# Row block 4 of a Gram matrix on column tiles, behind the K stage; z on four tiles of its own

## The chip, the cores and the metric

One core of a Trainium2 chip. The metric is the device time of one execution in microseconds (us). The profile shows one execution, by its span (about 1.7 us shorter than the time measured for the same execution).

## The reference, cut to what matters

`x` is 2048 x 576; its layer norm `xn` feeds an attention block without softmax and a gated feed-forward block, and both results are added to `x`:

```python
q, k, v = ...(xn @ wqkv)                         # 32 heads of 18
pq, pk = phi(q), phi(k)                          # phi(t) = (t + 1 if t > 0 else exp(t)) + 1e-6
kv = jnp.einsum("bhsd,bhse->bhde", pk, v)
z = jnp.einsum("bhsd->bhd", pk)                  # sums of pk over the sequence
num = jnp.einsum("bhqd,bhde->bhqe", pq, kv)
den = jnp.einsum("bhqd,bhd->bhq", pq, z)[..., None] + 1e-6
o = num / den                                    # then @ wo
return x + attention(xn) + (gelu(xn @ w_gate) * (xn @ w_up)) @ w_down
```

The kernel never forms `v`. It accumulates the Gram product `G = xn^T pk` (576 x 576) over the 16 sequence tiles and multiplies it by the v weights once, in the "kv stage". `z` is the column sum of `pk`.

## The kernel before

576 is 4.5 times 128, so G has four row blocks of 128 rows and a fifth, number 4, of 64. A column of ones appended to `xn` adds a 65th row to block 4, and that row is z. Blocks 0, 1 and 4 accumulate inside the K loop, block 2 behind it, and block 3 after q unit 12 (a q unit is five matmuls of 512 columns that make a piece of q, with the ScalarE and VectorE steps that follow):

```python
G_A = {
    0: [(0, 0, 0, 288), (1, 0, 288, 289)],          # (bank, first column in bank, first column of pk, width)
    1: [(2, 0, 0, 288), (3, 0, 288, 289)],
    4: [(0, 288, 0, 224), (1, 289, 224, 223), (2, 288, 447, 130)],
}
G_B = {2: [(5, 0, 0, 288), (6, 0, 288, 289)], 3: [(0, 0, 0, 288), (1, 0, 288, 289)]}

def g_accumulate(n, pieces):
    for kt, ps_ in pieces.items():
        j0, m = (kt * P, P) if kt < 4 else (D, HP + 1)
        for b, col, d0, w in ps_:
            nc.tensor.matmul(ps_all[:m, b, col:col + w], lhsT=xn[:, n, j0:j0 + m], rhs=pk[:, n, d0:d0 + w], ...)
# ... the K loop, which runs g_accumulate(n, G_A), cut ...
for n in range(NS):
    g_accumulate(n, {2: G_B[2]})
# ... copies of blocks 4, 0 and 1 out of PSUM, the remaining q steps, cut ...
q_unit(12)
# ...
for n in range(NS):
    g_accumulate(n, {3: G_B[3]})
g_copy(2, G_B, (nc.scalar, nc.vector))
g_copy(3, G_B, (nc.scalar, nc.vector))
q_unit(13)
z_stage(2, 3)      # 5 matmuls that spread z over the rows of zrep
kv_stage(6, 5)     # 25 matmuls: v weights times G
```

All products live in one tensor, `ps_all`, of 8 banks in PSUM, the memory that the matmuls write and the copies read. The layer that places the semaphores makes two engines that use the same bank take turns, whatever part of the bank each of them uses; the waits in the built programs show it.

Of the kernel before, what the change touches and what calls it, by code (L numbers as in the profile page):

```python
# [8 lines left out]
ACT = mybir.ActivationFunctionType  # L9
ALU = mybir.AluOpType  # L10
BF16 = mybir.dt.bfloat16
F32 = mybir.dt.float32
# [3 lines left out]
P = 128  # L16
HP = 64
S = 2048
D = 576
# [3 lines left out]
NS = S // P  # L23
# [4 lines left out]
HALF = D // 2  # L28
KT = 5
# [3 lines left out]
CR = 7 * DH  # L33
EPS_LN = 1e-5
EPS_ATT = 1e-6
# [2 lines left out]
WDS = 3  # L38
NWARM = 38
TD = 4  # L40
XW = 642
PKW = 578


class _Ring:
# [11 lines left out]
def kernel(  # L57
# [11 lines left out]
    nc = tc.nc  # L69
# [8 lines left out]
    const = ctx.enter_context(tc.tile_pool(name="const", bufs=1))  # L78
# [6 lines left out]
    ps_all = psum.tile([P, 8, 512], F32, name="ps_all")  # L85
# [10 lines left out]
    apool = attn_cm.__enter__()  # L96
# [5 lines left out]
    wqkv_sb = apool.tile([P, KT, 3 * D], BF16, name="wqkv_sb")  # L102
# [4 lines left out]
    def load_w(which, on=nc.sync):  # L107
        c = slice(which * D, (which + 1) * D)
        on.dma_start(wqkv_sb[:, 0:4, c], A_wqkv[0:512, c].rearrange("(kt p) c -> p kt c", p=P))
        on.dma_start(wqkv_sb[0:HP, 4, c], A_wqkv[512:576, c])  # L110
        if which == 0:
            on.dma_start(wq_lo[HP:P, :], A_wqkv[512:576, c])

    nc.scalar.preload_act_table_set("natural_log_exp_and_others")  # L114
    load_x(0, 1)
# [3 lines left out]
    nc.vector.memset(wqkv_sb[HP:P, 4, :], 0.0)  # L119
    nc.vector.memset(wqkv_sb[0:1, 0, D:D + 2], 0.0)  # L120
    load_w(1, nc.scalar)

    ident = const.tile([P, P], BF16, name="ident")
# [29 lines left out]

    pk = h_store[:, 0:NS * PKW].rearrange("p (n d) -> p n d", n=NS)
    wg_bufs = _Ring([fpool.tile([P, 4, GUB * P], BF16, name=f"wg{i}") for i in range(NWBUF)])
# [5 lines left out]
    def load_gu(i, part):  # L161
# [15 lines left out]


    xn = apool.tile([P, NS, XW], BF16, name="xn")
    nc.gpsimd.memset(xn[:, :, 640:641], 1.0)  # L180
    nc.gpsimd.memset(pk[:, :, D:D + 1], 1.0)

    bmask = const.tile([P, CR], F32, name="bmask")
    bm3 = bmask[:].rearrange("p (h e) -> p h e", e=DH)
# [2 lines left out]
        out=bm3, in_=bm3, compare_op=ALU.is_ge, fill=0.0,  # L187
# [3 lines left out]
        out=bm3, in_=bm3, compare_op=ALU.is_ge, fill=0.0,  # L191
        base=DH - 1, pattern=[[DH, 7], [0, DH]], channel_multiplier=-1,
    )
    g_sb = apool.tile([P, KT, D], BF16, name="g_sb")
    nc.gpsimd.memset(g_sb[HP:P, 4, :], 0.0)

    zsel = const.tile([P, CR], BF16, name="zsel")
    nc.gpsimd.memset(zsel[:], 0.0)
    nc.gpsimd.memset(zsel[HP:HP + 1, :], 1.0)

    mv = persist.tile([P, NS, nc.vector.BN_AGGR_DIM], F32, name="mv")
    rstd = persist.tile([P, NS], F32, name="rstd")
# [36 lines left out]
    def k_bank(n, hf):  # L239

        return hf if n == 1 else 5 + hf
# [9 lines left out]
    def phi_tile():  # L251
        return awork.tile([P, D], F32, name="phi_e", tag="phi_e", bufs=6)


    k_e = {}

    def k_part(n, hf):
        if n not in k_e:
            k_e[n] = phi_tile()
        hs = slice(hf * HALF, (hf + 1) * HALF)  # L260
        return ps_all[:, k_bank(n, hf), :HALF], k_e[n][:, hs], pk[:, n, hs]

    def k_relu(n, hf):
        ps, e, _ = k_part(n, hf)
        nc.scalar.activation(out=e, in_=ps, func=ACT.Relu, scale=-1.0)  # L265

    def k_exp(n, hf):
        _, e, _ = k_part(n, hf)
        nc.scalar.activation(out=e, in_=e, func=ACT.Exp, scale=-1.0)  # L269

    def k_sum(n, hf):
        ps, e, out_ = k_part(n, hf)
        nc.vector.scalar_tensor_tensor(out=out_, in0=ps, scalar=0.0, in1=e, op0=ALU.max, op1=ALU.add)  # L273
# [1 line left out]


    G_A = {
        0: [(0, 0, 0, 288), (1, 0, 288, 289)],
        1: [(2, 0, 0, 288), (3, 0, 288, 289)],
        4: [(0, 288, 0, 224), (1, 289, 224, 223), (2, 288, 447, 130)],  # L280
    }
    G_B = {2: [(5, 0, 0, 288), (6, 0, 288, 289)], 3: [(0, 0, 0, 288), (1, 0, 288, 289)]}
    eps_sum = const.tile([P, KT], F32, name="eps_sum")

    def g_accumulate(n, pieces):
        for kt, ps_ in pieces.items():
            j0, m = (kt * P, P) if kt < 4 else (D, HP + 1)
            for b, col, d0, w in ps_:
                nc.tensor.matmul(  # L289
                    ps_all[:m, b, col:col + w], lhsT=xn[:, n, j0:j0 + m], rhs=pk[:, n, d0:d0 + w],  # L290
                    start=(n == 0 and col == 0), stop=(n == NS - 1), skip_group_check=True,
                )



# [2 lines left out]
    LO, HI = slice(0, HP), slice(HP, P)  # L298
# [37 lines left out]
    def q_unit(i):  # L336
        sc, c = divmod(i, NCH)
        rows = DH * HCH[c]
        q0 = DH * HOFF[c]
        ps = ps_all[:rows, q_banks.next(), :]  # L340
        for kt in range(KT):
            nc.tensor.matmul(  # L342
                ps, lhsT=wqkv_sb[:, kt, q0:q0 + rows], rhs=xnT[:, kt, sc * SC:(sc + 1) * SC],
                start=(kt == 0), stop=(kt == KT - 1),
            )
        q_out[i] = ps
# [57 lines left out]
    def mask_pair(dst, b4, b1):  # L404

        nc.vector.tensor_tensor(
            out=dst[:CR, 0:4, :], in0=ps_all[:CR, b4, 0:4 * CR].rearrange("p (c d) -> p c d", c=4),
            in1=bmask[:CR, :].unsqueeze(1).to_broadcast([CR, 4, CR]), op=ALU.mult,
        )
        r4 = DH * HCH[4]  # L410
        nc.vector.tensor_tensor(
            out=dst[:r4, 4, :r4], in0=ps_all[:r4, b1, 0:r4], in1=bmask[:r4, :r4], op=ALU.mult,
        )

    def chunk_out(c, b4, b1):
        rows = DH * HCH[c]
        return ps_all[:rows, b4, c * CR:c * CR + rows] if c < 4 else ps_all[:rows, b1, 0:rows]

    def z_stage(b4, b1):
        for c in range(NCH):  # L420
            rows = DH * HCH[c]
            nc.tensor.matmul(
                chunk_out(c, b4, b1), lhsT=g_sb[:, 4, c * CR:c * CR + rows], rhs=zsel[:, :rows],
                start=(c in (0, 4)), stop=True, skip_group_check=True,
            )
        mask_pair(zrep, b4, b1)

    def kv_stage(b4, b1):

        for kt in (0, 1, 4, 2, 3):  # L430
            for c in range(NCH):
                rows = DH * HCH[c]
                nc.tensor.matmul(  # L433
                    chunk_out(c, b4, b1), lhsT=wqkv_sb[:, kt, 2 * D + c * CR:2 * D + c * CR + rows],
                    rhs=g_sb[:, kt, c * CR:c * CR + rows],
                    start=(kt == 0 and c in (0, 4)), stop=(kt == 3), skip_group_check=True,
                )
        mask_pair(kvT, b4, b1)

# [29 lines left out]
    def den_norm(sc, c, q, pieces):  # L469
# [30 lines left out]
        (lambda n: k_sum(n, 0), [9.00, 16.55, 13.07, 15.61, 18.43, 21.08, 23.93, 26.99, 30.05]),  # L500
        (lambda n: k_sum(n, 1), [10.83, 11.19, 13.68, 16.19, 18.79, 21.44, 24.29, 27.35, 30.41]),
        (lambda n: g_accumulate(n, G_A), [11.96, 17.36, 18.24, 20.21, 21.09, 23.07, 26.12, 29.18, 32.24]),
    ]

# [27 lines left out]
    todo += [(4.0, lambda n: nc.vector.memset(x_sb[0:1, n, 0:2], 0.0), 4)]  # L532
    todo += [(4.01, lambda n: load_x(n, 4), n) for n in (4,)]
    todo += [(4.02, lambda n: load_w(0), 0)] + [(4.03, lambda n: load_x(n, 4), n) for n in (8, 12)]
    todo.sort(key=lambda x: x[0])

# [2 lines left out]
        step(n)  # L539


    def g_copy(kt, pieces, on):

        m = P if kt < 4 else HP + 1
        eps = eps_sum[:m, kt:kt + 1]
        b, col, _, w = pieces[kt][-1]
        nc.vector.tensor_scalar_mul(out=eps, in0=ps_all[:m, b, col + w - 1:col + w], scalar1=EPS_ATT)
        for (b, col, d0, w), eng in zip(pieces[kt][::-1], on):
            w = min(w, D - d0)
            out_, in_ = g_sb[:m, kt, d0:d0 + w], ps_all[:m, b, col:col + w]  # L550
            if eng is nc.scalar:
                nc.scalar.activation(out=out_, in_=in_, func=ACT.Identity, bias=eps, scale=1.0)
            else:
                nc.vector.tensor_scalar_add(out=out_, in0=in_, scalar1=eps)


    load_w(2)
    for i in range(NWBUF):
        load_gu(i, 0)
        load_gu(i, 1)  # L560
    for n in range(NS):
        g_accumulate(n, {2: G_B[2]})
    g_copy(4, G_A, (nc.vector, nc.scalar, nc.vector))
    g_copy(0, G_A, (nc.scalar, nc.vector))
    g_copy(1, G_A, (nc.scalar, nc.vector))
    for _, step, n in todo[tail:]:
        step(n)
    q_unit(12)
    for step in (q_exp1, q_min, q_max):
        step(12)  # L570
    for n in range(NS):
        g_accumulate(n, {3: G_B[3]})
    g_copy(2, G_B, (nc.scalar, nc.vector))
    g_copy(3, G_B, (nc.scalar, nc.vector))
    q_unit(13)
    z_stage(2, 3)
    kv_stage(6, 5)
    for step in (q_exp1, q_min, q_max):
        step(13)
# [161 lines left out]
```

## Time and profile before

| what | before |
|---|---|
| time, first series | 523.57 us (523.47 to 523.83, 3 runs) |
| TensorE busy | 99% of the span |
| stage: end of q unit 11 to end of the kv stage | 53.20 to 65.78, 12.58 us |
| of it, 32 Gram matmuls behind the K loop, and 32 more behind q unit 12 | 4.00 us each |
| TensorE idle in the stage | none |

The stage is read from the chain of waits: the pieces of the chain in order of time, with start, length, engine, tile and line.

### The profile page before, as it was taken

What the parts mean: (1) busy time and instruction counts of PE and PEld (TensorE: products, weight loads), DVE (VectorE), ACT (ScalarE), POOL (GpSimd) and SP (SyncE); (2) the same over time, 40 slices, a digit from 0 to 9 for tenths busy, and PEclk for the clock granted to TensorE, in tenths of its full rate; (3) what the DMA queues carried; (4) which work ended last, traced back from release to release, by engine and by line L of the source; (5) the groups of instructions that cost most, each with busy time, mean ns of one, the idle gap of its engine ahead of it and who ended that gap; (6) DMA issues with size and microseconds to landing.
All of it is one profiled execution on the core that took longest, in us unless ns stands there. A gap on an engine that the chain in (4) does not pass through costs nothing.

```text
span 521.7 us, 10641 instructions
## 1 busy us (share of the span) xinstructions
PE 516.1 (99%) x4498; PEld 313.5 (60%) x4498; DVE 250.9 (48%) x436; ACT 143.1 (27%) x293; POOL 35.2 (7%) x55
## 2 busy tenths in 40 slices
PE   7999999999999999999999999999999999999997
PEld 6777755555587754444577744444777544445775
DVE  7996565876358323433388133333584233433101
ACT  6898442332320013323200032232000123322000
POOL 2021000211001100000012000000011000000000
PEclk9999999999999999999999999999999999999999
DMA  8334609899500045555300155555100355440000
GB/s 279 62 64 118 154 25 264 254 269 266 157 12 13 13 124 155 144 156 160 93 13 13 41 166 145 155 156 155 29 23 13 103 161 158 140 134 2 13 11 24
DMA packets 106282, 57.89 MB, mean 111 GB/s; under 512 B 13370, under 2 KB 105722, under 8 KB 106234
## 3 DMA queue, kind: packets, MB, share of 16 engines
q1 hardware_dynamic: 105626, 56.55, 38.8%
q8 instruction: 35, 0.57, 0.5%
q10 hardware_dynamic: 608, 0.66, 0.4%
q14 instruction: 13, 0.11, 0.1%
HBM read 52.86 MB, written 2.36 MB: 106 GB/s over the span
## 4 chain that ended last, share of the span: by engine, by line
PE 97%; DMA 1%; ACT 1%; DVE 0%; issue 0%
PE ps_all L313 55%; PE ps_all L677 27%; PE ps_all L289 4%; PE ps_all L682 4%; PE ps_all L245 3%; PE ps_all L342 3%; DMA wqkv_sb<-in_A_wqkv_dram 1%; PE ps_all L451 1%; PE ps_all L433 0%; PE ps_all L659 0%; ACT xnT L234 0%; ACT L114 0%; ACT phi_e L265 0%; ACT phi_e L269 0%; DVE hT L273 0%; DVE res L685 0%
## 5 line engine op out<-in xcount | busy, mean ns | idle before, releaser
L313 PE MATMUL ps_all<-xnT,wg 64*128 64x512 bf16 x1152 | 272.6, 376 | 0.0
L313 PE MATMUL ps_all<-xnT,wu 64*128 64x512 bf16 x1152 | 271.8, 376 | 0.0
L648 DVE TENSOR_TENSOR hT<-ps_all,gl 128x512 bf16<-128x512 f32 x144 | 99.5, 691 | 161.9 <-ACT gl L647 161.2
L647 ACT ACTIVATE gl<-ps_all 128x512 f32<-128x512 f32 x144 | 86.1, 598 | 314.3 <-PE ps_all L313 297.4
L313 PEld LDWEIGHTS <-wu 64*128 64x128 bf16 x1152 | 108.3, 94 | 66.3
L313 PEld LDWEIGHTS <-wg 64*128 64x128 bf16 x1152 | 108.3, 94 | 66.1
L677 PE MATMUL ps_all<-wd_sb,hT 128*128 128x288 bf16 x1152 | 147.0, 286 | 0.0
L677 PEld LDWEIGHTS <-hT 128*128 128x128 bf16 x1152 | 112.3, 98 | 30.6 <-issue 1.3
L475 DVE RECIPROCAL den_sb<-den_sb 126x128 f32<-126x128 f32 (+1 forms) x80 | 68.3, 911 | 0.5
L685 DVE TENSOR_TENSOR res<-ps_all,x_sb 128x288 bf16<-128x288 f32 x32 | 14.7, 458 | 88.0 <-PE ps_all L682 88.0
L313 PE MATMUL ps_all<-xnT,wr 64*128 64x512 bf16 x288 | 55.1, 376 | 0.0
L478 POOL TENSOR_TENSOR pqT<-pqT,den_sb 126x512 bf16<-126x512 bf16 (+3 forms) x25 | 24.2, 966 | 317.3 <-DVE den_sb L475 279.4
L682 PE MATMUL ps_all<-m_sb,pqT 126*128 126x288 bf16 (+1 forms) x160 | 24.9, 285 | 0.0
L313 PEld LDWEIGHTS <-wr 64*128 64x128 bf16 x288 | 14.4, 94 | 16.9 <-issue 0.7
L245 PE MATMUL ps_all<-wqkv_sb,xnT 128*128 128x288 bf16 x160 | 22.5, 286 | 0.9 <-DMA wqkv_sb<-in_A_wqkv_dram 0.8
L289 PE MATMUL ps_all<-hT,xn 128*128 128x288 bf16 (+4 forms) x176 | 22.4, 275 | 0.0
L289 PEld LDWEIGHTS <-xn 128*128 128x128 bf16 (+1 forms) x176 | 17.5, 102 | 4.1
L245 PEld LDWEIGHTS <-xnT 128*128 128x128 bf16 x160 | 15.4, 98 | 6.9 <-issue 1.4
L682 PEld LDWEIGHTS <-pqT 126*128 126x128 bf16 (+1 forms) x160 | 15.5, 97 | 4.1
L342 PE MATMUL ps_all<-xnT,wqkv_sb 128*126 128x512 bf16 (+1 forms) x70 | 17.4, 378 | 0.0
L273 DVE SCALAR_TENSOR_TENSOR hT<-ps_all,phi_e 128x288 bf16<-128x288 f32 x32 | 13.2, 450 | 4.6 <-ACT phi_e L269 4.0
L265 ACT ACTIVATE phi_e<-ps_all 128x288 f32<-128x288 f32 x32 | 12.9, 410 | 3.6 <-PE ps_all L245 2.1
(68 smaller groups left out, 173.8 us busy)
## 6 DMA issues: line engine op xcount, KB each, us to landing
wg<-in_B_w_gate_dram SPq DMA_DIRECT2D x72, 256.0 KB, 2.9
wu<-in_B_w_up_dram SPq DMA_DIRECT2D x72, 256.0 KB, 3.5
wd_sb<-in_B_w_down_dram SPq DMA_DIRECT2D x12, 432.0 KB, 4.6
wr<-in_B_w_gate_dram SPq DMA_DIRECT2D x72, 32.0 KB, 2.7
wr<-in_B_w_up_dram SPq DMA_DIRECT2D x72, 32.0 KB, 3.1
out_dram<-res SPq DMA_DIRECT2D x15, 144.0 KB, 1.8
x_sb<-in_A_x_dram SPq DMA_DIRECT2D x3, 576.0 KB, 7.1
wqkv_sb<-in_A_wqkv_dram SPq DMA_DIRECT2D x2, 576.0 KB, 4.7
```

The source lines that it names most:

```text
L245: nc.tensor.matmul(ps_all[:, k_bank(n, hf), :HALF], lhsT=xnT[:, kt, n * P:(n + 1) * P], rhs=wqkv_sb[:, kt, D + hf * HALF:D + (hf + 1) * HALF],
L273: nc.vector.scalar_tensor_tensor(out=out_, in0=ps, scalar=0.0, in1=e, op0=ALU.max, op1=ALU.add)
L289: nc.tensor.matmul(ps_all[:m, b, col:col + w], lhsT=xn[:, n, j0:j0 + m], rhs=pk[:, n, d0:d0 + w], start=(n == 0 and col == 0), stop=(n == ...
L313: return nc.tensor.matmul(self.outs[i], lhsT=self.lhs(i, rows, kt), rhs=self.rhs(i, rows, kt), start=start, stop=stop, skip_group_check=True,)
L342: nc.tensor.matmul(ps, lhsT=wqkv_sb[:, kt, q0:q0 + rows], rhs=xnT[:, kt, sc * SC:(sc + 1) * SC], start=(kt == 0), stop=(kt == KT - 1),)
L475: nc.vector.reciprocal(out=d[:, h:h + P], in_=d[:, h:h + P])
L478: nc.gpsimd.tensor_tensor(out=pqT[:rows, c, cols], in0=pqT[:rows, c, cols], in1=d, op=ALU.mult)
L647: nc.scalar.activation(out=gl[:], in_=ps_all[:, b[0], :], func=ACT.Gelu_apprx_tanh)
L648: nc.vector.tensor_tensor(out=hT[:, GUB * k + i, :], in0=ps_all[:, b[1], :], in1=gl[:], op=ALU.mult)
L677: nc.tensor.matmul(acc, lhsT=hT[:, f, j * P:(j + 1) * P], rhs=wd_sb[:, f, hs], start=(f == 0), stop=False,)
L682: nc.tensor.matmul(acc, lhsT=pqT[:rows, c, ts_], rhs=m_sb[:rows, c, hs], start=False, stop=(c == NCH - 1),)
L685: nc.vector.tensor_tensor(out=res[:, hs], in0=acc, in1=x_sb[:, n, hs], op=ALU.add)
```

## The change

Block 4 uses half of the array's columns (64 of 128) at full price. The change takes it out of the K loop, puts block 2 in its place, and computes block 4 behind q unit 12 on two 64-column tiles of the array, one for each half of pk's 576 columns. (A column tile is a block of the array's columns that is given its own weights and its own matmuls.) The ones row no longer fits, so z gets 64 matmuls of its own on four 32-column tiles, one for each quarter of pk's columns.

```diff
-    4: [(0, 288, 0, 224), (1, 289, 224, 223), (2, 288, 447, 130)],
+    2: [(0, 288, 0, 224), (1, 289, 224, 223), (2, 288, 447, 132)],
 ...
+def g_last(bank):
+    for n in range(NS):
+        for hf in range(2):
+            nc.tensor.matmul(
+                ps_all[hf * HP:(hf + 1) * HP, bank, 0:HALF + 1], lhsT=xn[:, n, 4 * P:4 * P + HP],
+                rhs=pk[:, n, PK0[hf]:PK0[hf] + HALF + 1], ...)
+def z_sums(bank):
+    for n in range(NS):
+        for g in range(4):
+            p0 = PK0[g // 2] + (g % 2) * DQ
+            nc.tensor.matmul(
+                ps_all[g * ZQ:(g + 1) * ZQ, bank, 0:DQ], lhsT=z_ones[:], rhs=pk[:, n, p0:p0 + DQ], ...)
+def z_copies(bank):
+    for g in range(4):
+        r = slice(g * ZQ, (g + 1) * ZQ)
+        out_, in_ = z_sb[r, g * DQ:(g + 1) * DQ], ps_all[r, bank, 0:DQ]
+        # odd g: nc.scalar.activation(...), even g: nc.vector.tensor_scalar_add(...)
 ...
 q_unit(12)
-for n in range(NS):
-    g_accumulate(n, {3: G_B[3]})          # block 3 now stands where block 2 stood, behind the K loop
-g_copy(2, G_B, (nc.scalar, nc.vector))
-g_copy(3, G_B, (nc.scalar, nc.vector))
+g_last(0)
+z_sums(1)
+g_copy(3, (6, 288), [(ALL, 6, 0, 288, 288, nc.scalar), (ALL, 5, 0, 0, 288, nc.vector)])
+g_copy(4, (0, 288), [(HI, 0, 0, 288, 288, nc.scalar), (LO, 0, 0, 0, 288, nc.vector)])
+z_copies(1)
 q_unit(13)
 z_stage(2, 3)
 kv_stage(6, 5)
```

Cut: the layout of pk (a column of ones for each half), the pieces of block 2's copies, memsets for the zero halves of G's block 4 and for z, one more 72 KB load of v weights, the z stage's operands (it reads `z_sb` now, and `zsel` has four rows of ones instead of one), and the kv stage's order of blocks (0, 1, 4, 2, 3 before, 0 to 4 after).

## The prediction

> **What bounds the kernel now.** I read the page from the top: busy shares (part 1), then the chain that ended last (part 4), then the chain of waits in order of time between 50 and 68 us, where the change lies, then the timeline and the groups by form there.
>
> ```profile
> span 521.7 us, 10641 instructions
> PE 516.1 (99%) x4498; PEld 313.5 (60%) x4498; DVE 250.9 (48%) x436; ACT 143.1 (27%) x293; POOL 35.2 (7%) x55
> ...
> PE 97%; DMA 1%; ACT 1%; DVE 0%; issue 0%
> ```
>
> TensorE is the bound from end to end: 99% busy and 97% of the chain. A change pays only by shortening TensorE's own stream, and costs as soon as TensorE waits. The granted clock is 1.00 in every window I asked for. The chain around the change, kernel before:
>
> ```profile
> 52.12 1.08 PE ps_all L342 x5
> 53.20 4.75 PE ps_all L289 x39
> 57.95 1.08 PE ps_all L342 x5
> 59.02 4.00 PE ps_all L289 x32
> 63.02 1.08 PE ps_all L342 x5
> 64.10 0.26 PE ps_all L422 x5
> 64.36 1.43 PE ps_all L433 x25
> ```
>
> Columns: start, length, engine, line. L289 is the Gram product, L342 a q unit, L422 the z stage, L433 the kv stage. The 39 are the last sequence tile's 7 in-loop pieces (0.75 us, as each tile's x7 row shows) and 32 matmuls of row block 2; the 32 at 59.02 are row block 3. Nothing stands between the pieces: there is no wait in 53.20 to 65.78. Two blocks of 32 at 4.00 us each are 125 ns per matmul of 288 or 289 columns, or N/2.4 + about 4.6 ns, N the columns.
>
> Row block 4 has 64 rows plus a row of ones for z (128x65 weights), yet its 577 columns pass in the K loop at full price: 16 x 577/2.4 = 3.85 us with half of the array unused. That is what the change is after.
>
> What the evacuations cost, from the timeline and the groups by form of 50 to 66 us:
>
> ```profile
> 63.06 0.16 DVE L547 TENSOR_SCALAR eps_sum<-ps_all 128x1 f32<-128x1 f32 x1 [1.53 <-PE ps_all L289]
> ...
> 63.25 0.50 ACT L552 ACTIVATE g_sb<-ps_all,eps_sum 128x288 bf16<-128x288 f32 x1 [1.75 <-DVE eps_sum L547]
> 63.25 0.52 DVE L554 TENSOR_SCALAR g_sb<-ps_all,eps_sum 128x288 bf16<-128x288 f32 x1
> ```
> ```profile
> L552 ACT ACTIVATE g_sb<-ps_all,eps_sum 65x223 bf16<-65x223 f32 x1 | 0.4, 445 | 0.8 <-DVE eps_sum L547 0.8
> ...
> L554 DVE TENSOR_SCALAR g_sb<-ps_all,eps_sum 65x129 bf16<-65x129 f32 x1 | 0.3, 348 | 0.0
> ```
>
> The reader is to see that the last Gram matmul lands at 63.02, both copies run side by side from 63.25 (two different banks), and are done by 63.77, before the q unit that covers them ends at 64.10. The z stage's data (row block 4) had been copied 9 us earlier, so it waits for nothing.
>
> **What the Trainium skill says.** (1) "TensorEngine Tiling (Array Packing)", Key Properties: tiles work independently and in parallel, but changing the tiling mode drains the engine. The trace of before has row tiles only, and agrees for them: two 64-row matmuls of 512 columns start at 65.71 and 65.72, and the pairs follow every 0.21 us. No column tile is in it. (2) Same page, Restrictions: column tiling disables the fast weight load. In the trace 128-column loads take 98 ns, 126-column ones 136, 65-column ones 111; the difference of 38 ns is what loading 126 columns instead of 32 would cost at 2.4 per ns. So I put a 64-column load at 27 ns and a 32-column one at 13 ns (estimates): two of the first (53) fit under 120 ns of streaming, four of the second (53) under 60. (3) "TensorE: Matmul & The Clock Gate", "Wait — 56ns, not 53.3ns?": starts of matmuls are never closer than about 25 ns. Row-tile pairs starting 10 ns apart speak against that between tiles; a steady stream of short ones is not in the trace. (4) "PSUM — Partial Sum Buffer", "PSUM bank collisions raise a hardware error": two engines may not use one bank and quadrant at once, and guarding by the whole bank is the simple version. Before keeps the two copies in two banks, and they start together (63.25).
>
> **The change part by part.**
> *In the K loop*: row block 2 takes block 4's place, 579 columns for 577, 16 x 2/2.4 = 0.01 us. Block 3 takes block 2's place behind the loop (4.00 us, same banks). No change to 59.02.
> *Removed*: the 4.00 us of 32 matmuls behind q unit 12.
> *Added, Gram rows*: 32 matmuls of 289 columns on two 64-column tiles. Side by side a pair takes 289/2.4 + 4.6 = 125 ns: 16 x 125 = 2.00 us.
> *Added, z*: 64 matmuls of 144 columns in 16 groups of four. Side by side, 64 + a few ns a group: 1.04 us. With a start every 25 ns (the skill's figure), 64 x 25 = 1.6 us. Each of these 64 also signals its semaphore, which makes me choose 1.6.
> *Mode switches*: 128 to 64 to 32 and back to 128 columns. The nearest thing in the trace is row tiles to full array at 255.5, where the first 36 matmuls take 4.52 instead of 4.41 us: 0.1 each, of which I count 0.3 in all.
> *Sum on TensorE alone*: -4.00 + 2.00 + 1.6 + 0.3 = -0.1 us (with fast z, -0.66).
>
> *The copies*: here I expect the gain to go. The built program shows what each copy waits for. The two halves of block 4 now share one bank and are chained: sum (DVE), then ScalarE's half, then VectorE's half. The four z copies share one bank too and are chained DVE, ACT, DVE, ACT. The z stage, next after q unit 13, needs all four. In time: Gram rows land at 59.02 + 2.00 + 0.1 = 61.12. DVE has q unit 12's two operations until about 60.9 and block 3's copy to 61.55 (before had the same work at 60.82 to 61.53). Then sum 0.15, ACT 0.50, DVE 0.52, with 0.03 us per hop (eps_sum ending 54.55, copy starting 54.58): end at 62.78. z lands at 61.12 + 1.6 + 0.1 = 62.82 (62.3 if fast, still behind the copies). A z copy of 144 columns: on DVE 348 + 15 x 1.07 = 0.36 us (slope from 129 and 288 columns), on ACT 0.38 (slope from 223 and 288). Chain: 2 x 0.36 + 2 x 0.38 + 3 x 0.03 = 1.57, so 64.43. TensorE's load follows 0.05 us later, and the last two matmuls of the z stage land some 0.35 us after that: 64.85. In before the z stage ended at 64.36. q unit 13 ends near 64.0, so TensorE idles about 0.5 us. The kv stage stands behind z in the same queue and cannot fill it.
>
> *Net*: +0.5 us at the kv stage, and everything behind is TensorE's own stream (0.0 idle before L313 in the groups), so it moves whole: 523.57 + 0.5 = **524.1 us**.
>
> *Elsewhere*: one more 72 KB load of weights (before's sister loads land in 4.3 us, some 10 us early) and half a microsecond of issue; hidden. More GpSimd memsets at the start: before ends them at 3.62 and copies the first duplicate at 5.82. I add about 1.4 us (z_sb like g_sb's 0.57, the small ones 0.1 to 0.3), so 5.0: still before 5.82.
>
> **Rivals.** *A, the chain is shorter than I think* (short copies, hops overlapping): then TensorE alone decides, -0.1 to -0.66, about 523.2. For it: TensorE's sum; against: the explicit DVE-ACT-DVE-ACT order. *B, column tiles do not run together*, or weight loads hold each tile up: Gram rows 4.0, and z 64 x 64 ns = 4.1 us, so +4.4 and a chain tail of about 0.7: 528.7. For it: no column tile in the trace; against: the row tiles, and 53 ns of loads fitting. A half-way case (z alone slow, at 60 ns each) gives z 3.9 us: about 526.5. *C, the memsets delay the first duplicate*, which the first transposes need: up to 0.5 us more, if they cost twice my estimate.
>
> **Range and chances.** Centre +0.5. A takes the low end to 523.2, the half-way case of B the high end to 526.0. A 2% change is 10.5 us, more than the whole 4.00 us block could give or than B costs; neither end is reachable by this stage alone.
>
> **What will show it.** In the chain: 32 Gram matmuls in about 2.0 to 2.1 us (4.0 is B); 64 z matmuls in 1.0 to 1.7; an idle of about 0.5 us of TensorE before the z stage, released by ACT's z copy; the four z copies strictly in turn; the kv stage beginning near 64.85; the span from there to the end as before (457.3 us). If the idle is absent, the copy chain is the wrong step; if the Gram or z time is large, the concurrency is; if the first K matmuls start later than 7.41, the memsets are.

## The result, and the profile after

| | before | after |
|---|---|---|
| time, first series | 523.52 us (523.07 to 523.83, 4 runs) | 523.94 us (523.36 to 524.54, 4 runs) |
| stage, end of q unit 11 to end of kv | 12.58 us | 12.58 us |
| span of the profiled run | 521.7 us | 521.8 us |

The ratio is 1.0009, with a 95% interval of 0.9991 to 1.0026: the same.

The page of the changed kernel, the lines for span, busy shares and the chain by engine:

```profile
span 521.8 us, 10779 instructions
PE 516.3 (99%) x4562; PEld 313.8 (60%) x4562; DVE 251.2 (48%) x438; ACT 143.8 (28%) x296; POOL 36.4 (7%) x62
...
PE 96%; ACT 1%; DMA 1%; DVE 1%; issue 0%; ACTq 0%
```

Only the last line tells of a change: TensorE's share of the chain fell from 97 to 96%, and ACT and DVE now carry a piece of it. The chain of waits of the changed kernel shows which piece (L303 is the Gram product, L387 the q units, L439 to L447 the ACT and DVE steps of q unit 12, L595 and L597 the copies of G, L335 and L337 those of z, L467 the z stage, L477 the kv stage, L358 what follows):

```profile
53.03 4.72 PE ps_all L303 x39
57.75 1.09 PE ps_all L387 x5
...
58.93 0.60 ACT phi_e L439
...
59.56 0.44 DVE phi_e L443
...
60.02 0.69 DVE pqT L447
...
60.81 0.52 DVE g_sb L597
...
61.43 0.51 ACT g_sb L595
...
61.96 0.51 DVE g_sb L597
62.47 0.22 DVE z_sb L337
...
62.71 0.38 ACT z_sb L335
...
63.11 0.32 DVE z_sb L337
...
63.45 0.38 ACT z_sb L335
...
63.88 0.30 PE ps_all L467 x2
64.18 1.43 PE ps_all L477 x25
65.61 77.21 PE ps_all L358 x714
```

Where before's chain had one unbroken line of TensorE, this one leaves TensorE at 58.84 and runs through ACT and DVE for 5 us: first q unit 12's own steps (to 60.71), then block 3's copy, the two halves of block 4 one after the other (61.43 and 61.96), and then the four z copies DVE, ACT, DVE, ACT, each starting within 0.03 us of the end of the one before it (the chain counts that gap as issue). TensorE comes back at 63.88. Block 3's copy stands behind q unit 12's two steps in DVE's queue, by the order in which the kernel records them, though TensorE had finished block 3 at 57.75; no run recorded it earlier. What TensorE did meanwhile is in the timeline of the changed kernel (start, length, engine, line, operation, and the idle before it in brackets):

```profile
58.76 2.17 PE L312 MATMUL ps_all<-hT,xn 128*64 128x289 bf16 x32
...
60.86 1.20 PE L325 MATMUL ps_all<-hT,z_ones 128*32 128x144 bf16 x64
...
61.98 1.29 PE L387 MATMUL ps_all<-xnT,wqkv_sb 128*126 128x512 bf16 x5
...
63.88 0.17 PEld L467 LDWEIGHTS <-z_sb 128*126 128x126 bf16 x2 [0.27 <-ACT z_sb L335]
```

The 32 Gram matmuls take 2.10 us from start to start (60.86 - 58.76) and the 64 for z take 1.12. q unit 13 ends at 61.98 + 1.29 = 63.27, and the last two z-stage loads come at 63.88. So 3.36 us of work (2.10 + 1.12, and 0.14 by which q unit 13 is longer than its usual 1.08) stands for the 4.00 us removed, a gain of 0.64 us, and 0.61 us passes waiting for the last z copy. The three z-stage matmuls whose copies came earlier run inside that time. Before had z and kv right behind the q unit. The last 0.03 us are in what is left of the z stage, 0.30 us instead of 0.26. The sum is 12.58 us in both.

The two stages begin 0.17 us apart (53.20 and 53.03), because the first weights landed 0.15 us sooner (the load's piece of the chain ends at 7.37 and 7.22). From the end of the kv stage to the last addition before the output it is 453.02 us before (65.78 to 518.80) and 453.01 after: between these two, nothing is given back later. Behind the last addition, where the output is written, the profiled execution of after is 0.2 us longer; no run looked into that.

### The profile page after: what moved, and what is told of

It reads as the page before. It is cut to its first block, busy times and chain, and to the rows that moved or that the text cites. A ratio compares the mean times of both kernels' runs of the same rounds, so it can differ in the third digit from the quotient of the medians.

```text
span 521.8 us, 10779 instructions
## 1 busy us (share of the span) xinstructions
PE 516.3 (99%) x4562; PEld 313.8 (60%) x4562; DVE 251.2 (48%) x438; ACT 143.8 (28%) x296; POOL 36.4 (7%) x62
## 4 chain that ended last, share of the span: by engine, by line
PE 96%; ACT 1%; DMA 1%; DVE 1%; issue 0%; ACTq 0%
PE ps_all L358 55%; PE ps_all L724 27%; PE ps_all L729 4%; PE ps_all L259 3%; PE ps_all L303 3%; PE ps_all L387 3%; DMA wqkv_sb<-in_A_wqkv_dram 1%; PE ps_all L495 1%; PE ps_all L477 0%; PE ps_all L706 0%; ACT xnT L248 0%; ACT L116 0%; DVE g_sb L597 0%; ACT phi_e L279 0%; ACT z_sb L335 0%; DVE pqT L447 0%
## 5 line engine op out<-in xcount | busy, mean ns | idle before, releaser
L358 PE MATMUL ps_all<-xnT,wg 64*128 64x512 bf16 x1152 | 272.7, 376 | 0.0
L358 PE MATMUL ps_all<-xnT,wu 64*128 64x512 bf16 x1152 | 271.8, 376 | 0.0
L358 PEld LDWEIGHTS <-wu 64*128 64x128 bf16 x1152 | 108.3, 94 | 66.2
L358 PEld LDWEIGHTS <-wg 64*128 64x128 bf16 x1152 | 108.3, 94 | 66.0
L358 PE MATMUL ps_all<-xnT,wr 64*128 64x512 bf16 x288 | 55.2, 376 | 0.0
L358 PEld LDWEIGHTS <-wr 64*128 64x128 bf16 x288 | 14.5, 94 | 16.8 <-issue 0.7
L303 PE MATMUL ps_all<-hT,xn 128*128 128x288 bf16 (+4 forms) x144 | 18.2, 273 | 0.0
L387 PE MATMUL ps_all<-xnT,wqkv_sb 128*126 128x512 bf16 (+1 forms) x70 | 17.4, 379 | 0.0
L303 PEld LDWEIGHTS <-xn 128*128 128x128 bf16 x144 | 13.9, 98 | 3.3
```

Of the source, the lines that this page charges most:

```text
L303: nc.tensor.matmul(ps_all[:, b, col:col + w], lhsT=xn[:, n, kt * P:(kt + 1) * P], rhs=pk[:, n, p0:p0 + w], start=(n == 0 and col == 0), st ...
L358: return nc.tensor.matmul(self.outs[i], lhsT=self.lhs(i, rows, kt), rhs=self.rhs(i, rows, kt), start=start, stop=stop, skip_group_check=True,)
L387: nc.tensor.matmul(ps, lhsT=wqkv_sb[:, kt, q0:q0 + rows], rhs=xnT[:, kt, sc * SC:(sc + 1) * SC], start=(kt == 0), stop=(kt == KT - 1),)
```

## The experiments

Each edit is on top of the changed kernel unless said. All results were correct. The stage is the one of the tables above.

### The changed kernel again

No edit. The four times of the first series had lain in two groups.

> The changed kernel once more, beside the kernel before on the same chip, because its four times lay in two groups about 1 us apart (523.4 and 524.5) while its stage from the end of q unit 11 to the end of the kv stage took 12.58 us in both profiles. Theory (the gain on TensorE, about 0.6 us, is taken back by an idle of about 0.6 us before the z stage, net 0): ratio to before 1.000, and the groups 1 us apart are found with the kernel before as well. Rival (the change itself costs some 0.4 us outside the stage, as the medians say): ratio 1.001, and only the changed kernel has the slower group.

Measured: 523.73 us (523.55 to 524.48, 6 runs) against 523.68 us for the kernel before on the same chip (523.20 to 525.63, 11 runs); ratio 0.9998 (0.9984 to 1.0012). The stage is 12.58 us again (52.96 to 65.54). The kernel before has longer executions too (524.47, 524.72, 525.63). So the 0.42 us between the first medians is no more than this spread. In the stage the change costs nothing and gains nothing; in the time, the interval leaves room for 0.8 us less to 0.6 us more.

### kv before z

```diff
+    kv_stage(6, 5)
     z_stage(2, 3)
-    kv_stage(6, 5)
```

> One edit: the kv stage is recorded before the z stage, so that TensorE has 25 matmuls (1.43 us) to do while the four z copies take their turns. Theory (the chain of z copies is what holds TensorE): the idle before the z stage is gone, kv begins right after q unit 13, and the stage from the end of q unit 11 to the end of the last of z and kv takes 12.0 us instead of 12.58; the kernel 0.55 to 0.65 us less than the changed one. Rival (the idle belongs to something else that comes just as late, such as row block 4's copy or VectorE's queue): kv now waits instead of z, and the stage stays within 0.2 us of 12.58.

Measured: the chain of waits of this kernel is TensorE alone again.

```profile
58.85 2.10 PE ps_all L312 x32
60.95 1.12 PE ps_all L325 x64
62.08 1.22 PE ps_all L387 x5
63.30 1.40 PE ps_all L477 x25
64.70 0.28 PE ps_all L467 x5
64.98 2.13 PE ps_all L358 x16
```

kv starts as q unit 13 ends, and z follows with its copies long done. The stage is 53.05 to 64.98, 11.93 us: 0.65 less than before or after. The copies themselves are as slow as ever (the last z copy runs from 63.48 to 63.85 in this kernel's timeline), but nobody waits for them. The rival falls: no other late operand takes the place of z. Time: 523.23 us (523.14 to 524.28, 6 runs), ratio 0.9991 (0.9975 to 1.0006), which does not exclude 1. In the profiled execution 0.28 us of the gain was lost again behind the stage: from its end to the last addition it is 453.30 us (64.98 to 518.28), where before and after have 453.02 and 453.01.

### z in two banks

The order of the stages stays, and only the turns are taken away.

```diff
-    ps_all[g * ZQ:(g + 1) * ZQ, bank, 0:DQ], lhsT=z_ones[:], ...
+    ps_all[g * ZQ:(g + 1) * ZQ, bank[g % 2], 0:DQ], lhsT=z_ones[:], ...
-    out_, in_ = z_sb[r, g * DQ:(g + 1) * DQ], ps_all[r, bank, 0:DQ]
+    out_, in_ = z_sb[r, g * DQ:(g + 1) * DQ], ps_all[r, bank[g % 2], 0:DQ]
-    z_sums(1)   z_copies(1)
+    z_sums((1, 4))   z_copies((1, 4))
```

> One edit: z groups 1 and 3 accumulate in bank 4 instead of bank 1, so that ScalarE's two copies and VectorE's two read different banks and are no longer chained; the order of the stages stays. Theory (the turns on one bank make the chain): the two ScalarE copies start right after the last z matmul lands, the two VectorE copies right after row block 4's copy, all four are done before q unit 13 ends, and the stage takes 12.0 us. Rival (the copies are late because their engines are busy, not because they take turns): the last copy still ends more than 0.4 us behind q unit 13 and the stage stays near 12.5 us.

Measured, timeline of this kernel:

```profile
62.12 1.29 PE L387 MATMUL ps_all<-xnT,wqkv_sb 128*126 128x512 bf16 x5
62.26 0.77 ACT L335 ACTIVATE z_sb<-ps_all,eps_z 32x144 bf16<-32x144 f32 x2 [0.20 <-PE ps_all L325]
62.52 0.62 DVE L337 TENSOR_SCALAR z_sb<-ps_all 32x144 bf16<-32x144 f32 x2
63.03 0.50 PEld L467 LDWEIGHTS <-z_sb 128*126 128x126 bf16 x5
```

ACT's two copies run together with DVE's two, and all end by 63.14, before q unit 13 does at 63.41. z loads are pulled ahead without a wait. The stage is 53.17 to 65.09, 11.92 us. The copies and engines are the same as in the changed kernel; only the bank differs. That shows the cause: not the copies' length, but the turns on one bank. Time: 523.01 us (522.48 to 523.56, 6 runs), ratio 0.9981 (0.9967 to 0.9995).

The same kernel was run once more on another chip:

> The kernel with z in two banks once more, on this chip, since single times spread by over 1 us. Theory: stage 11.92 us again, 0.65 us under the kernel before in the profile, ratio near 0.9988. Rival (the earlier ratio of 0.9981 was mostly spread): ratio within 0.0005 of 1.

Measured: the stage is 11.93 us (54.61 to 66.54), but the time was 523.65 us (523.14 to 525.27, 5 runs), ratio 1.0004 (0.9991 to 1.0017). The stage came out as the theory says, and the ratio as the rival says. The profiled execution was the slowest of the five, and its chain of waits shows where an execution can lose over a microsecond. First this run, then the earlier run of the same kernel:

```profile
1.96 5.87 DMA wqkv_sb<-in_A_wqkv_dram
...
7.87 1.36 PE ps_all L259 x5
```
```profile
1.96 5.39 DMA wqkv_sb<-in_A_wqkv_dram
...
7.39 0.79 PE ps_all L259 x5
```

The first weights landed 0.48 us later, the first five K matmuls then took 1.36 us instead of 0.79, and the K stage ended 1.44 us later (54.61 against 53.17). Read in windows, the trace of this run has a granted clock of 0.50 from 7.87 to 10.75 and 1.00 from 11.38 on; the earlier run has 1.00 from 5.00 to 9.50. TensorE had been idle for 1.37 us before these matmuls here, and for 0.86 us in the earlier run. That the longer idle let the clock fall is my reading of these lines; no run tested it. Another 0.85 us went behind the stage (453.87 us from its end to the last addition, against 453.02), where the chain runs through the DMA queue and the load of `wo` (78.61, 7.92 us long). Either way, this spread lies outside the stage, is larger than 0.65 us, and makes single ratios of 0.1% unreliable.

### Both halves of block 4 on one column tile

```diff
-    ps_all[hf * HP:(hf + 1) * HP, bank, 0:HALF + 1], lhsT=xn[:, n, 4 * P:4 * P + HP],
+    ps_all[0:HP, bank[hf], 0:HALF + 1], lhsT=xn[:, n, 4 * P:4 * P + HP],
-    g_last(0)
+    g_last((0, 3))
-    [(HI, 0, 0, 288, 288, nc.scalar), (LO, 0, 0, 0, 288, nc.vector)]
+    [(LO, 3, 0, 288, 288, nc.scalar), (LO, 0, 0, 0, 288, nc.vector)]
     # and the memset of block 4's zero rows, to fit
```

> The two halves of row block 4 both go to the same 64-column tile (outputs on partitions 0 to 63 of banks 0 and 3), everything else as in the changed kernel. It measures what the second column tile is worth. Theory (matmuls on two column tiles run side by side, one after the other on one tile): the 32 Gram matmuls take 4.0 us instead of 2.10. Rival (the saving comes from the shorter weights or the narrower tile, not from running side by side): they stay near 2.1 us.

Measured, chain of waits of this kernel:

```profile
59.22 4.12 PE ps_all L311 x32
```

4.12 us against 2.10: two 64-column tiles do run side by side, at 1.96 times the rate of one. The stage is 14.32 us (53.42 to 67.74). It grew by 1.74 and not by 2.02, because the wait for z is shorter: q unit 13 ends at 65.69 and the last z loads come at 66.01, 0.32 us instead of 0.61. The Gram rows now take so long that DVE has done its earlier work; it had been idle for 0.55 us when z landed, and the four z copies began at once (64.51). Block 4's two copies, in two banks here, start together (63.45 and 63.51), where they take turns in the changed kernel.

### All of z on one column tile

```diff
-    ps_all[g * ZQ:(g + 1) * ZQ, bank, 0:DQ], lhsT=z_ones[:], ...
+    ps_all[0:ZQ, bank[g // 2], (g % 2) * DQ:(g % 2 + 1) * DQ], lhsT=z_ones[:], ...
     # two copies of 288 columns instead of four of 144; z_sums((1, 4)), z_copies((1, 4));
     # one row of ones in zsel, and start= for the first matmul of each bank
```

> All four quarters of z on the same 32-column tile (outputs on partitions 0 to 31 of banks 1 and 4, two copies instead of four). It measures what three more tiles are worth. Theory (one tile takes its matmuls one after the other at N/2.4 + 4.6 ns): the 64 z matmuls take 64 x 65 = 4.1 us instead of 1.12. Rival (starts are limited to one per about 16 ns by something else than the tiles): clearly less than 4 us.

Measured, chain of waits of this kernel:

```profile
61.26 4.20 PE ps_all L325 x64
```

4.20 us against 1.12, 3.75 times. The stage is 15.00 us (53.37 to 68.37) with no wait for z in it: 3.08 more than z in two banks.

### Gram pair and z in turn

```diff
-    g_last(0)
-    z_sums(1)
+    for n in range(NS):
+        g_last(0, [n])
+        z_sums(1, [n])
```

> The changed kernel, with the Gram pair and the four z matmuls of each sequence tile recorded in turn, so that the tiling mode changes 32 times instead of 2 in the 96 matmuls. Theory (0.1 us for each change of mode): 30 more changes make the 96 matmuls take about 3.2 + 3.0 = 6.2 us. Rival (the 0.1 us seen at the borders comes from filling after a dependence or from a slow first load, not from the mode): they take about 3.2 us as before.

Measured, chain of waits of this kernel, the first of sixteen turns:

```profile
58.99 0.24 PE ps_all L312 x2
59.23 0.18 PE ps_all L325 x4
```

From the first Gram start to q unit 13's first start, in the timeline, the 96 matmuls take 6.73 us (58.92 to 65.65) instead of 3.22 (58.76 to 61.98). That is 3.51 us for 30 more changes of tiling mode, 0.12 us each. So the 0.1 us at the borders goes with the mode. The stage is 16.76 us (53.19 to 69.95).

### Block 4 on four column tiles as well

On top of z in two banks:

```diff
-    for hf in range(2):
-        ... ps_all[hf * HP:(hf + 1) * HP, bank, 0:HALF + 1], lhsT=xn[:, n, 4 * P:4 * P + HP], ...
+    for g in range(4):
+        hf, rr = divmod(g, 2)
+        ... ps_all[g * 32:(g + 1) * 32, bank, 0:HALF + 1],
+            lhsT=xn[:, n, 4 * P + rr * 32:4 * P + (rr + 1) * 32], ...
```

> On top of the edit with z in two banks: row block 4 on four 32-column tiles (each half of the columns twice, 32 rows each), so that the Gram rows and z use one tiling mode and one of the three mode changes goes. The candidate to beat both kernels. Theory (each change of tiling mode costs TensorE about 0.1 us, and four tiles stream 289 columns side by side as two do): Gram rows about 2.1 us, z about 1.02 instead of 1.12, the stage 11.8 us against 11.92 with z in two banks, and the kernel some 0.7 us below the kernel before. Rival (the 0.1 us belongs to any new set of tiles or to filling the array, not to the mode): stage stays at 11.92.

Measured, chain of waits of this kernel:

```profile
59.04 2.09 PE ps_all L313 x63
61.13 1.03 PE ps_all L326 x64
62.16 1.22 PE ps_all L388 x5
```

Twice as many Gram matmuls (64; one record is missing) take the same 2.09 us, and z drops from 1.12 to 1.03, since the mode no longer changes between them. The stage is 11.83 us (53.24 to 65.07), 0.75 less than before. Time: 523.24 us against 523.78 (5 and 9 runs), ratio 0.9994 (0.9980 to 1.0008). It was run once more:

> The candidate once more, for its time on another set of executions: in the profile its stage was 0.75 us shorter than that of the kernel before, which is 0.14% of the time, as much as the half-width of the interval. Theory (the 0.75 us reach the end, as TensorE is the bound behind the stage): ratio near 0.9986, stage 11.83 us. Rival (something behind the stage takes it back): the part from the end of the kv stage to the last result is longer than the 453 us of the other profiles and the ratio is 1.

Measured: the stage is 11.83 us again (53.64 to 65.47), the time 523.23 us (522.68 to 523.65, 5 runs) against 523.84 (9 runs), ratio 0.9989 (0.9975 to 1.0003). From the end of the stage to the last addition it is 453.01 us in the first run and 453.23 in the second, so in these two nothing behind the stage takes the gain back by more than 0.2 us; kv before z lost 0.28 there and the second run of z in two banks 0.85. In the trace this version beats both kernels in its stage; in the time, both ratios lie below 1 but neither interval excludes it.

| version | stage, us | against before |
|---|---|---|
| before; after; after again | 12.58; 12.58; 12.58 | 0.00 |
| kv before z | 11.93 | -0.65 |
| z in two banks, twice | 11.92; 11.93 | -0.66; -0.65 |
| and block 4 on four tiles, twice | 11.83; 11.83 | -0.75 |
| block 4 on one tile | 14.32 | +1.74 |
| z on one tile | 15.00 | +2.42 |
| Gram pair and z in turn | 16.76 | +4.18 |

## Why the prediction was right or wrong

**The time** of 523.94 us against 524.1 predicted lies in the range, and so does the median of the later series (523.73); a change of 2%, called out of reach, did not come. But that it came so near to 524.1 is luck: the 0.42 us between the first medians is within the spread that the repeat shows, and not the +0.5 us that I had worked out. The difference is 0.00 in the stage. (The range's upper end, 526.0, also lay below the 526.5 of the case that it was to cover.)

**The bound and the place**: right. TensorE is the bound, the K loop did not change (4.72 and 4.75 us for the 39 matmuls there), and what stands behind the stage did not either, up to the last addition; from the start of kv to the end of the span it is 457.6 us, predicted 457.3.

**Gram rows**, 2.00 us side by side and 0.1 for the mode: right, 2.10. One tile takes 4.12, so rival B (no concurrency) falls. The 2.4 columns per ns of the sums come out of before's chain: a K matmul of 288 columns takes 123 ns (1.23 us for 10) and a q matmul of 512 takes 216 (1.08 us for 5), which is 224 more columns in 93 ns.

**Mode switches**, 0.3 us in all: right. The borders show 0.10, 0.09 and 0.14 (2.10, 1.12 and 1.22 us against 2.00 as worked out, 1.03 without the change of mode, and 1.08 for the usual q unit), and the run with 30 more puts one at 0.12.

**z**, "With a start every 25 ns (the skill's figure), 64 x 25 = 1.6 us": wrong. It took 1.12 with its mode change and 1.03 without one, which is 16 ns per start. I had both figures and chose the wrong one, for a reason that does not hold: I wrote that each of the 64 signals its semaphore, but in the trace of the changed kernel one of them does, the last. This made my sum on TensorE -0.1, and it was -0.64. I had given -0.66 as the fast case.

**The copies taking turns**: the mechanism is right, and two experiments show it, one that leaves the turns and lets TensorE do other work, and one that takes the turns away. The size was off. With 0.17 us added to after's times, so that both stages begin together, block 4's second copy ended at 62.64, predicted 62.78. The first z copy was taken up as it ended, where I had waited for z to land at 62.82 and added a hop. The four copies took 1.37 us and not 1.57: those on DVE took 0.28 and 0.30 us (timeline) where I had 0.36 from wider tiles. The end, 0.05 + 0.35, was 0.34 in all. Together: 0.22 for the start of the four copies (62.86 to 62.64), 0.20 for their length and 0.06 for the end, 0.48 in all, from 64.83 to 64.35; the prediction wrote 64.85, but its own terms (64.43 + 0.05 + 0.35) make 64.83. The step "Net: +0.5 us at the kv stage" is the one that failed, by this term.

**The two errors do not add.** The wait for z begins with the copies and not with TensorE, so a faster z only lengthens the idle: predicted 0.5, measured 0.61. In the prediction z landed at 62.82 and block 4's copies ended at 62.78, so that mis-sizing z by half a microsecond moved the start of the z copies by less than 0.1 us; it had said of fast z "still behind the copies".

**Rival A**, a shorter chain after which TensorE alone decides, is what the edited kernels became, at -0.65 us. **Rival C**: the memsets ended at 5.06, predicted 5.0, and the first duplicate began at 5.63; they delay nothing.

## What to carry to other kernels

When work is moved later on the engine that bounds the kernel, the copies of its result move later too: look for what covered them before, and record an independent stage in front of the one that needs them. If two engines share the copying and their waits go by bank, as here, give each a bank of its own; on one bank, four copies became a chain of four turns. Small products on column tiles are worth it (nearly 2 and 4 times here), if the tiling mode changes seldom.

## What the Trainium skill lacked or had wrong

- "TensorE: Matmul & The Clock Gate", "Wait — 56ns, not 53.3ns?": starts never below about 25 ns, without a word on tiles. On four 32-column tiles 64 matmuls of 144 columns took 1.03 us, 16 ns each, each with its own weight load, so the floor does not hold across tiles. The same page has about 4 ns for each further tile under "Measured speedup vs the span model", which the prediction did not use.
- "TensorEngine Tiling (Array Packing)", Key Properties: a change of mode drains the engine, but no cost is given. 30 more changes cost 3.51 us, 0.12 each.
- The same page, Restrictions: column tiling disables the fast weight load, without a number there. 64-column loads took 106 to 111 ns and 32-column ones 91 to 98, against 98 for a full one in before's trace, and neither showed in the pace.
- "PSUM — Partial Sum Buffer", "PSUM bank collisions raise a hardware error": it calls guarding by bank the simple version, but not what it costs. Four copies from four separate quadrants of one bank took 1.37 us in turn, and 0.88 us (62.26 to 63.14) from two banks.
